# Row maxima of a routed attention in steps of 256 and 512 keys, with VectorE's queue rearranged

## The chip, the core and the metric

The kernel runs on one core of one Trainium2 chip. The metric is the device time of one execution in microseconds (us). A core has five engines that run their own queues side by side: TensorE (PE in the profile, its weight loads PEld), VectorE (DVE), ScalarE (ACT), GpSimd (POOL) and SyncE (SP, which starts transfers). They meet at semaphores. TensorE writes its results into PSUM, eight banks of 512 float32 for each of the 128 partitions; VectorE and ScalarE read PSUM and may write it.

## The reference

Two blocks follow each other. The first is an attention over 4 batches of 8 heads with 768 positions of 64 values, in which a query sees only the keys that were assigned to the same one of 16 clusters:

```python
q_assign = np.argmax(np.einsum('bhsd,hcd->bhsc', q_n, c_n), axis=-1)
k_assign = np.argmax(np.einsum('bhsd,hcd->bhsc', k_n, c_n), axis=-1)
mask = q_assign[:, :, :, None] == k_assign[:, :, None, :]
scores = scale * np.matmul(q, k.transpose(0, 1, 3, 2))
scores = np.where(mask, scores, -1000000000.0)
scores = scores - np.max(scores, axis=-1, keepdims=True)
attn = np.exp(scores)
attn = attn / (np.sum(attn, axis=-1, keepdims=True) + 1e-09)
return np.matmul(attn, v).astype(np.float32)
```

The second takes the result as 3072 tokens of 512 values and computes `h = x @ w_in` (512 to 2048), `g = h * erf(softplus(h))` and `g @ w_out`. The change touches the attention alone.

## The kernel before

The 32 heads are worked as 16 pairs (`p` = 0 to 15), two heads side by side in the partitions 0 to 63 and 64 to 127. A pair has 12 units: two halves of 384 queries, each with six blocks `j` of 128 keys. A unit takes scores (keys by queries) in float32, adds mask and shift, takes the exponential and multiplies by v. `period(p, i)`, line 1345, with `i` = 0 to 5, issues the work of two units `u` and `u + 1`, and between them the preparations of later pairs. Periods 0 to 2 are the first half of the queries, 3 to 5 the second. All engines' instructions keep the order in which the program issues them, so the order of the calls in `period` is the order of every queue.

What runs in a period, with the names that the profile shows:

- `step_ahead(u)` (line 1332) runs the first of two steps of the row maxima of a coming half, `maxima_step` (463). A step takes 128 queries `t` of both heads against half of the 768 keys: two bf16 passes on TensorE into the two banks of the tile `wide` (`wide<-kv,qv`, then the mask `wide<-km,qm`), then one reduction on VectorE, `nmx<-wide`. Both steps use the same `wide`, so each waits until VectorE has read the one before. The second step of a period, `step_ahead(u + 1, True)`, is a generator: its first pass stands behind the products, its mask pass between the two units' `scores`.
- `products(u)` (514) multiplies q and k in float32 into a score bank pair, `sc<-qT,kT`; there are two such pairs, for u and u + 1. `scores(u)` (527) adds mask and shift, `sc<-qm,km`; `curve(u)` (541) takes the exponential on ScalarE, `pr<-sc`.
- `attend(w)` (562) multiplies the exponentials of the two units before by v, `turned<-pr,in_v`, 16 matmuls a unit, into the first 386 columns of `turned[0]` (first half) or `turned[1]` (second half). `accumulate` (550) sums the exponentials on GpSimd.
- `divide` (575), after a half's last unit (at the end of periods 0 and 3): TensorE sums over the keys into the other `turned` bank (`turned<-more_out,minus`), ScalarE makes the inverse (`inv`, twice), VectorE refines it (`den`), scales the two parts of the result (`turned<-turned,inv`, twice, here raw 0 and raw 1), makes the output `x` (`more_out<-den,turned`), and SyncE stores it. It is a generator, `part[0]`, moved on by `next` in the period that follows.
- Routing of pair p + 2: in period 3, `similarities` (394) multiplies by the centroids into `turned[1]` (`turned<-...,ccT`), then `choose` (407), a generator in `routing[0]`, works on VectorE: transposition `sims<-turned`, maximum over the 16 clusters `mx` (384 values to 24; before, into the columns 488 to 511 of the score bank of unit u + 1: `sc<-sims`), comparison `hot<-sims,sc`, and the transpositions `aside` and `hotT`.
- `masks` (437) spreads the clusters of the next pair by a matmul with `pick` into a `turned` bank and copies them to `qm` and `km`; `turn` (494) puts the row maxima in.
- A weight tile of the second block is made a pair at a time between: `size`, `rest` and `sign` on ScalarE, `bounded` and `shifted` on VectorE (`w_in<-w_in` or `w_out<-w_out`), `summed` on GpSimd.

The tiles of the result of `attend` and of the maximum of `choose` are made and taken so:

```python
turned = [ps.tile([P, 512], F32, name=f"turned{i}") for i in range(2)]   # line 172
mx = (wide[:, 0] if spare is None else spare)[:, 512 - n :]              # line 417
```

After the attention (about 408 us) the second block runs to the end; it has no part in the change.

Of the kernel before, what the change touches and what calls it, by code (L numbers as in the profile page):

```python
# [14 lines left out]
ALU = mybir.AluOpType  # L15
ACT = mybir.ActivationFunctionType
AX = mybir.AxisListType
PSUM = bass.MemoryType.PSUM

P = 128  # L20
B, H, S, D = 4, 8, 768, 64
# [4 lines left out]
HW = S // 2  # L26
QW = HW // 2
TW = QW + 1
HJ = NJ // 2
HP = H // 2  # L30
NPAIR = B * HP
DM, DFF = H * D, 2048
NFT = DFF // P
# [9 lines left out]
BIG = 2.0**60  # L43
# [3 lines left out]
N_LATE = 4  # L47
PLACE_OF = [n % 5 for n in range(25)] + [2, 3, 2]
LAST_X = 11
MASKS = {(0, 2): ("k", 0), (2, 0): ("q", 0), (2, 2): ("k", 1), (5, 2): ("q", 1)}  # L50
FIRST_MASKS = {(2, 0): ("k", 0), (2, 1): ("q", 0), (2, 2): ("k", 1), (5, 2): ("q", 1)}

KAPPA = {1: (0, 1), 2: (0, 0), 0: (1, 1), 3: (1, 0)}
# [93 lines left out]
def kernel(  # L147
# [24 lines left out]
    turned = [ps.tile([P, 512], F32, name=f"turned{i}") for i in range(2)]  # L172
# [149 lines left out]
    def bounded(n):  # L322
        w = w_steps[n][0]
        ve.tensor_scalar(out=w, in0=w, scalar1=2.0, scalar2=None, op0=ALU.max)

    def sign(n):
        hi, _, upper = steps[n]
        ae.activation(out=upper, in_=hi, func=ACT.Prelu, scale=2.0**-25, alpha=2.0**90)

    def shifted(n):  # L330
        w = w_steps[n][0].bitcast(U32)
        ve.tensor_scalar(out=w, in0=w, scalar1=3, scalar2=None, op0=ALU.logical_shift_left)
# [8 lines left out]
    for e in range(2):  # L341
        for n in range(2):
            r = e * D + n * Q
# [90 lines left out]
        if p < NPAIR:  # L434
            ae.copy(out=pairs[p][nm + "v"], in_=pairs[p][nm + "T"])

    def masks(p, nm, half, bank, narrow=False, copied_by=ae):

        if p >= NPAIR:
            return lambda: None  # L440
        st = pairs[p]
        cols = slice(half * HW, (half + 1) * HW)
        r, hot = slice(0, D) if nm == "q" else slice(D, P), st["hotT"]
        picked = pick[r, half]
        if narrow:
            r = slice(r.start + Q, r.stop)
            picked = pick[r, 1]
            hot = hot if half else st["aside"]
        won = bank[:, 0:HW]
        te.matmul(won, lhsT=picked, rhs=hot[r], start=True, stop=True)  # L450
        if nm == "q":
            return lambda: ae.activation(out=st["qm"][:, cols], in_=won, func=ACT.Relu)
        if copied_by is ve:
            return lambda: ve.tensor_scalar(
                out=st["km"][:, cols], in0=won, scalar1=BIG, scalar2=nbig, op0=ALU.mult, op1=ALU.add
            )
        return lambda: ae.activation(
            out=st["km"][:, cols], in_=won, func=ACT.Identity, bias=nbig, scale=BIG
        )
# [3 lines left out]
    def maxima_step(p, i, sm=wide, behind=False):  # L463

        st = pairs[p]
        nmx = maxima[p % 2]
        t, half = divmod(i, 2)

        def passes(a, b, start, rows):
            for e in range(2):  # L470
                r = slice(e * D + rows.start, e * D + rows.stop)
                te.matmul(
                    sm[:, e, 0:HW], lhsT=st[a][r, t * P : (t + 1) * P],
                    rhs=st[b][r, half * HW : (half + 1) * HW], start=start, stop=not start,
                )

        passes("qv", "kv", True, slice(0, D))
        if behind:
            yield
        passes("qm", "km", False, slice(Q, D) if behind else slice(0, D))  # L480
        if behind:
            yield
        ve.tensor_reduce(
            out=nmx[:, :, t, half], in_=sm[:, :, 0:HW], axis=AX.X, op=ALU.max, negate=True
        )
        if i in (NJ - 1, 2 * NJ - 1):
            h = i // NJ
            ve.tensor_reduce(
                out=lowest[h][:, :, ::D].rearrange("p t e -> p e t"),
                in_=nmx[:, :, h * HJ : (h + 1) * HJ], axis=AX.X, op=ALU.min,  # L490
            )
            turns.append((p, h))
# [21 lines left out]
    def products(u):  # L514
        p, half, j = units[u]
        if u in sc_of:
            return
        st = pairs[p]
        sc = sc_of[u] = ps_s.tile([P, 2, 512], F32, name="sc", tag="s")
        for e in range(2):  # L520
            r = slice(e * D, (e + 1) * D)
            te.matmul(
                sc[:, e, 0:HW], lhsT=st["kT"][r, j * P : (j + 1) * P],
                rhs=st["qT"][r, half * HW : (half + 1) * HW], start=True, stop=False,
            )
# [49 lines left out]
    def divide(u):  # L575

        p, half, _ = units[u]
        st = pairs[p]
        av = st["av", half]

        psum = turned[1 - half][:, 0:QW]
        for g in range(4):
            te.matmul(psum[g * Q : (g + 1) * Q], lhsT=minus, rhs=st["acc", half][:, g], start=True, stop=True)

        if u + 1 < len(units):
            inv = routep.tile([P, QW], F32, name="inv")
            den = routep.tile([P, QW], F32, name="den")
        else:
            inv, den = part_of(0, 4 * HW, QW), part_of(1, 0, QW)
        ae.activation(out=inv, in_=psum, func=ACT.Ln, bias=alleps, scale=-1.0)  # L590
        ae.activation(out=inv, in_=inv, func=ACT.Exp, scale=-1.0)
        yield
        ve.scalar_tensor_tensor(
            out=den, in0=psum, scalar=S * EPS, in1=inv, op0=ALU.subtract, op1=ALU.mult
        )
        for k in range(2):
            raw = av[:, k, 0:QW]
            ve.scalar_tensor_tensor(
                out=raw, in0=raw, scalar=av[:, k, QW : QW + 1], in1=inv, op0=ALU.add, op1=ALU.mult
            )  # L600
        yield
        x = part_of(0, (2 * p + half) % 4 * HW, HW).rearrange("p (k x) -> p k x", k=2)
        ve.scalar_tensor_tensor(
            out=x, in0=den.unsqueeze(1).to_broadcast([P, 2, QW]), scalar=2.0, in1=av[:, :, 0:QW],
            op0=ALU.add, op1=ALU.mult,
        )
        b, r = divmod(p, HP)
        for g in range(4):
            rows_of, at = r * P + g // 2 * D, b * S + half * HW + g % 2 * QW
            nc.sync.dma_start(  # L610
                out=x_dram[rows_of : rows_of + D, at : at + QW].rearrange("(k r) x -> r k x", k=2),
                in_=x[g * Q : (g + 1) * Q],
            )
        if half == 1:
            del pairs[p]
        yield
# [715 lines left out]
    def step_ahead(u, behind=False):  # L1332
        p, i = divmod(u + NJ, 2 * NJ)
        steps = maxima_step(p, i, behind=behind) if p < NPAIR else iter(())
        if not behind:
            run(steps)
        return steps
# [7 lines left out]
    def period(p, i):  # L1345
# [4 lines left out]
        def mask(place):  # L1350
            which = (MASKS if p else FIRST_MASKS).get((i, place))
            if which:
                return masks(p + 1, *which, turned[0 if i in (0, 5) else 1], place > 1, ve if i == 0 else ae)
            return lambda: None

        if u > 0:
            for which in turns if i in (0, 3) else ():
                turn(*which)
                turns.remove(which)
            step_ahead(u)  # L1360
        mask(0)()
        next(part[0], None)
        if i == 5:
            next(routing[0], None)
# [2 lines left out]
        if u == 2:  # L1367
            next(routing[0])
        products(u)
        products(u + 1)  # L1370
        mask(1)()
        second = step_ahead(u + 1, True) if u > 0 else iter(())
# [1 line left out]
        rows = D if u == 0 or u + NJ >= len(units) else Q  # L1374
        scores(u, rows)
        next(second, None)
        if i:
            next(second, None)
        next(part[0], None)
        scores(u + 1, rows)  # L1380
        later = mask(2)
        if i == 0:
            later()
            later = lambda: None
            next(second, None)
        if i == 3:
            similarities(p + 2)
            routing[0] = choose(p + 2, sc_of[u + 1][:, 0], True)
        curve(u)
        later()  # L1390
        curve(u + 1)
# [8 lines left out]
        if i == 0 and early(n1 - 1):  # L1400
            bounded(n1 - 1)
            shifted(n1 - 1)
            sign(n1 - 1)
        elif i == 1 and early(n1):
            size_and_rest(n1)
        elif i == 3 and early(n1):
            bounded(n1)
            sign(n1)
        elif i == 5 and early(n2):
            rest(n2)  # L1410
        for _ in range(min(len(forms), FORMS.get(p, {}).get(i, 0))):
            forms.pop(0)[0]()
        if i == 3:
            next(routing[0], None)
            if early(n1):
                shifted(n1)
            for _ in range(2):
                next(routing[0], None)
        elif i == 1:
            load(p + 1, "v", v, vp)  # L1420
            if p == 0:
                run(routing[0])
                transposes(2, "q")
        elif i == 2:
            transposes(p + 2, "k")
        elif i == 4:
            vectors(p + 2, "k")
            vectors(p + 2, "q")
        elif i == 5:
            transposes(p + 3, "q")  # L1430
# [222 lines left out]
```

## Time and profile before

| | us |
|---|---|
| median of 3 runs (959.59 to 960.75) | 959.68 |
| the profiled execution, own time | 959.94 |
| its span, first to last instruction | 958.1 |
| the attention, 18 to 408 us of the span | 390.00, of it PE busy 389.26, DVE 330.22, ACT 295.33, POOL 317.90 |
| the second block, 408 to 958 us | 550.00, of it PE busy 546.26 |
| one pair, 250.56 to 275.21 and 275.21 to 299.68 us | 24.65 and 24.47, PE busy all of it |
| granted TensorE clock | 1.00 |

The span is counted from the first to the last instruction; the execution's own time is 1.8 us longer. A busy PE in this table means that a matmul was under way somewhere in the array; several run side by side in its row groups of 32 or 64 rows, and one may wait while another ends, so small waits don't show as idle time but as a wider distance between starts. The windows of 250.56, 275.21 and 299.68 us are the starts of three period 3s. The periods' lengths in the pair from 250.56 us, by the starts of their first `wide<-kv,qv`: period 3 4.91 (4.73 in most pairs), period 4 3.82, period 5 3.92, period 0 4.09, period 1 3.83, period 2 4.09.

### The profile page before, as it was taken

What the parts mean: (1) busy time and instruction counts of PE and PEld (TensorE: products, weight loads), DVE (VectorE), ACT (ScalarE), POOL (GpSimd) and SP (SyncE); (2) the same over time, 40 slices, a digit from 0 to 9 for tenths busy, and PEclk for the clock granted to TensorE, in tenths of its full rate; (3) what the DMA queues carried; (4) which work ended last, traced back from release to release, by engine and by line L of the source; (5) the groups of instructions that cost most, each with busy time, mean ns of one, the idle gap of its engine ahead of it and who ended that gap; (6) DMA issues with size and microseconds to landing.
All of it is one profiled execution on the core that took longest, in us unless ns stands there. A gap on an engine that the chain in (4) does not pass through costs nothing.

```text
span 958.1 us, 22447 instructions
## 1 busy us (share of the span) xinstructions
PE 950.1 (99%) x8954; PEld 728.2 (76%) x8954; DVE 798.0 (83%) x1395; ACT 539.0 (56%) x815; POOL 538.7 (56%) x375
## 2 busy tenths in 40 slices
PE   8999999999999999999999999999999999999998
PEld 3555555555555555588888888998999899989987
DVE  8888888888888887787689889788868987897887
ACT  3777777777777777542524531654257236625541
POOL 1688888778888888897669910360054016202600
PEclk9999999999999999999999999999999999999999
DMA  9345545544454522041403454463445336343533
GB/s 224 61 112 112 112 111 112 112 112 111 90 117 84 132 56 56 22 152 55 177 1 154 154 164 138 135 202 110 155 125 174 115 128 210 110 149 119 157 115 110
DMA packets 172313, 116.06 MB, mean 121 GB/s; under 512 B 131376, under 2 KB 141104, under 8 KB 172208
## 3 DMA queue, kind: packets, MB, share of 16 engines
q1 hardware_dynamic: 169280, 113.41, 42.3%
q8 instruction: 71, 1.16, 0.5%
q10 hardware_dynamic: 2928, 1.21, 0.4%
q14 instruction: 34, 0.28, 0.1%
HBM read 90.21 MB, written 24.38 MB: 120 GB/s over the span
## 4 chain that ended last, share of the span: by engine, by line
PE 95%; DVE 2%; ACT 1%; DMA 1%; issue 0%; DVEq 0%; SPq 0%; ACTq 0%
PE bank L138 41%; PE turned L138 32%; PE sc L138 17%; PE wide L138 6%; DVE nmx L138 1%; DMA out_dram<-osb 0%; ACT a_s L138 0%; DVE osb L138 0%; ACT L138 0%; DVE g L138 0%; DMA in_q<-in_q_dram 0%; DVE g_more L138 0%; DVE kT L138 0%; DVE sims L138 0%; DVE qT L138 0%
## 5 line engine op out<-in xcount | busy, mean ns | idle before, releaser
L138 POOL TENSOR_TENSOR more_out<-more_out,pr 128x768 f32<-128x768 f32 x128 | 217.3, 1698 | 16.2 <-ACT pr L138 6.7
L138 DVE TENSOR_REDUCE nmx<-wide 128x2 f32<-128x768 f32 x189 | 180.5, 955 | 46.4 <-PE wide L138 45.9
L138 ACT ACTIVATE pr<-sc 128x768 f32<-128x768 f32 x192 | 148.7, 810 | 87.2 <-PE wide L138 68.6
L138 POOL TENSOR_TENSOR g<-g 128x512 f32<-128x512 f32 x36 | 47.2, 1310 | 216.6 <-DVE g L138 214.7
L138 PE MATMUL turned<-pr,in_v 128*32 128x193 f32 x3072 | 144.8, 330 | 0.0
L138 PEld LDWEIGHTS turned<-pr,in_v 128*32 128x32 f32 x3072 | 91.5, 109 | 50.7 <-issue 21.3
L138 PE MATMUL sc<-qT,kT 64*128 64x384 f32 x528 | 98.3, 486 | 0.0
L138 DVE TENSOR_TENSOR g<-g 128x512 f32<-128x512 f32 x114 | 79.0, 693 | 15.2 <-PE bank L138 11.7
L138 DVE TENSOR_TENSOR g<-a_s,g 128x512 f32<-128x512 f32 x80 | 73.5, 944 | 5.6 <-ACT a_s L138 5.6
L138 DVE TENSOR_TENSOR g<-bank,g 128x256 f32<-128x256 f32 (+1 forms) x129 | 63.8, 522 | 15.3 <-PE bank L138 8.1
L138 PE MATMUL bank<-w_out,g 128*128 128x256 f32 x328 | 75.4, 379 | 0.0
L138 ACT ACTIVATE a_s<-g 128x1024 f32<-128x1024 f32 (+1 forms) x36 | 41.0, 1149 | 55.9 <-POOL g L138 45.3
L138 PE MATMUL bank<-g_more,g 128*128 128x256 f32 x304 | 71.8, 379 | 0.0
L138 PE MATMUL bank<-x_own,w_in 128*128 128x128 f32 (+1 forms) x432 | 71.6, 308 | 0.0
L138 POOL TENSOR_TENSOR more_out<-pr,pr 128x768 f32<-128x768 f32 x32 | 58.9, 1839 | 20.1 <-ACT pr L138 20.1
L138 PEld LDWEIGHTS bank<-w_out,g 128*128 128x128 f32 x328 | 62.3, 190 | 8.5
L138 PEld LDWEIGHTS <-qv 64*128 64x128 bf16 x384 | 26.9, 93 | 53.4 <-issue 37.3
L138 PEld LDWEIGHTS sc<-qT,kT 64*128 64x128 f32 x528 | 49.2, 187 | 21.9 <-ACT inv L138 3.1
L138 ACT ACT_TABLE_LOAD x40 | 51.3, 1283 | 24.4 <-DVE g L138 23.7
L138 PE MATMUL wide<-kv,qv 64*128 64x384 bf16 x378 | 63.9, 328 | 1.1 <-ACT km L138 0.6
L138 PEld LDWEIGHTS bank<-x_own,w_in 128*128 128x128 f32 x432 | 61.1, 191 | 4.0 <-issue 0.6
L138 PEld LDWEIGHTS bank<-g_more,g 128*128 128x128 f32 x304 | 57.8, 190 | 7.9
(242 smaller groups left out, 2065.3 us busy)
## 6 DMA issues: line engine op xcount, KB each, us to landing
g_more<-b_dram SPq DMA_DIRECT2D x48, 512.0 KB, 3.5
g_more<-w_dram SPq DMA_DIRECT2D x84, 256.0 KB, 2.8
x_own<-in_moe_w_in_dram SPq DMA_DIRECT2D x13, 512.0 KB, 5.4
in_v<-in_v_dram SPq DMA_DIRECT2D x32, 192.0 KB, 3.3
x_dram<-more_out SPq DMA_DIRECT2D x128, 48.0 KB, 1.7
x_own<-x_dram SPq DMA_DIRECT2D x6, 1024.0 KB, 5.4
in_k<-in_k_dram SPq DMA_DIRECT2D x59, 96.0 KB, 2.7
in_q<-in_q_dram SPq DMA_DIRECT2D x58, 96.0 KB, 4.9
```

Source lines behind the costliest of these rows:

```text
L138: ins = getattr(self.engine, name)(*args, **kw)
```

## The change

The 768 keys of a row are no longer cut at 384. For the rows `t` = 0, 1, 3 and 4 the first step takes 256 keys and the second 512, for `t` = 2 and 5 they take 352 and 416. Work moves in VectorE's queue: the copy of one mask (`km`, period 0) goes to ScalarE, raw 1 of the division goes behind the second maximum, the comparison `hot` goes from period 3 to period 4, `bounded` in period 3 behind the transposition `sims`. On ScalarE, `sign` of period 0 goes ahead of the period's exponentials. One mask matmul of period 2 goes from ahead of the products to between them. The maximum `mx` of `choose` is put into `turned[0]`, columns 488 to 511, in place of the score bank.

```diff
+KEYS = (S - 512, S - 512, 352)
...
-MASKS = {(0, 2): ("k", 0), (2, 0): ("q", 0), (2, 2): ("k", 1), (5, 2): ("q", 1)}
+MASKS = {(0, 2): ("k", 0), (2, 3): ("q", 0), (2, 2): ("k", 1), (5, 2): ("q", 1)}
...
-    def masks(p, nm, half, bank, narrow=False, copied_by=ae):
+    def masks(p, nm, half, bank, narrow=False):
...
-        if copied_by is ve:
-            return lambda: ve.tensor_scalar(
-                out=st["km"][:, cols], in0=won, scalar1=BIG, scalar2=nbig, op0=ALU.mult, op1=ALU.add
-            )
         return lambda: ae.activation(
             out=st["km"][:, cols], in_=won, func=ACT.Identity, bias=nbig, scale=BIG
         )
...
         t, half = divmod(i, 2)
+        first = KEYS[t % HJ]
+        keys = (slice(0, first), slice(first, S))[half]
+        n = keys.stop - keys.start
...
                 te.matmul(
-                    sm[:, e, 0:HW], lhsT=st[a][r, t * P : (t + 1) * P],
-                    rhs=st[b][r, half * HW : (half + 1) * HW], start=start, stop=not start,
+                    sm[:, e, 0:n], lhsT=st[a][r, t * P : (t + 1) * P],
+                    rhs=st[b][r, keys], start=start, stop=not start,
                 )
...
-            out=nmx[:, :, t, half], in_=sm[:, :, 0:HW], axis=AX.X, op=ALU.max, negate=True
+            out=nmx[:, :, t, half], in_=sm[:, :, 0:n], axis=AX.X, op=ALU.max, negate=True
...
                 out=raw, in0=raw, scalar=av[:, k, QW : QW + 1], in1=inv, op0=ALU.add, op1=ALU.mult
             )
-        yield
+            if k == 0:
+                yield
...
-                return masks(p + 1, *which, turned[0 if i in (0, 5) else 1], place > 1, ve if i == 0 else ae)
+                return masks(p + 1, *which, turned[0 if i in (0, 5) else 1], place == 2)
...
+            if i == 0 and early(n1 - 1):
+                sign(n1 - 1)
             step_ahead(u)
         mask(0)()
+        if i == 4:
+            next(routing[0], None)
         next(part[0], None)
...
         products(u)
+        mask(3)()
         products(u + 1)
         mask(1)()
...
         next(second, None)
-        if i:
-            next(second, None)
+        next(second, None)
         next(part[0], None)
         scores(u + 1, rows)
         later = mask(2)
         if i == 0:
             later()
             later = lambda: None
-            next(second, None)
         if i == 3:
             similarities(p + 2)
-            routing[0] = choose(p + 2, sc_of[u + 1][:, 0], True)
+            routing[0] = choose(p + 2, turned[0], True)
...
         if i == 0 and early(n1 - 1):
             bounded(n1 - 1)
             shifted(n1 - 1)
-            sign(n1 - 1)
...
         elif i == 3 and early(n1):
-            bounded(n1)
             sign(n1)
...
         if i == 3:
             next(routing[0], None)
             if early(n1):
+                bounded(n1)
                 shifted(n1)
-            for _ in range(2):
-                next(routing[0], None)
+            next(routing[0], None)
```

## The prediction

> **What bounds the kernel now.** I read the page first, then the chain of waits and the two engines' timelines of one pair of heads. The page:
>
> ```profile
> PE 950.1 (99%) x8954; PEld 728.2 (76%) x8954; DVE 798.0 (83%) x1395; ACT 539.0 (56%) x815; POOL 538.7 (56%) x375
> ...
> PE 95%; DVE 2%; ACT 1%; DMA 1%; issue 0%; DVEq 0%; SPq 0%; ACTq 0%
> ```
>
> TensorE is busy 99% of the span and is 95% of the chain that ended last. So a microsecond counts only if it shortens TensorE's stream or makes TensorE wait; work taken from VectorE (83%) counts for nothing by itself. TensorE in period 3 of one pair (its timeline):
>
> ```profile
> 275.21 0.34 PE L138 MATMUL wide<-kv,qv 64*128 64x384 bf16 x2
> 275.38 0.33 PE L138 MATMUL wide<-km,qm 64*128 64x384 bf16 x2
> 275.55 1.45 PE L138 MATMUL sc<-qT,kT 64*128 64x384 f32 x8
> 276.84 0.33 PE L138 MATMUL wide<-kv,qv 64*128 64x384 bf16 x2
> 277.10 0.33 PE L138 MATMUL sc<-qm,km 32*128 32x384 bf16 x2
> 277.10 0.34 PE L138 MATMUL wide<-km,qm 32*128 32x384 bf16 x2
> 277.27 0.32 PE L138 MATMUL sc<-qm,km 32*128 32x384 bf16 x2
> ...
> 278.19 1.49 PE L138 MATMUL turned<-pr,in_v 128*32 128x193 f32 x32
> 279.50 0.51 PE L138 MATMUL turned<-more_out,minus 128*32 128x192 f32 x8
> 279.94 0.34 PE L138 MATMUL wide<-kv,qv 64*128 64x384 bf16 x2
> ```
>
> Read the starts. The first maxima pass takes 0.17 us to the next start, so does the mask pass. At 277.10 the mask pass of the second step starts together with the first unit's scores: they lie in different row groups. The `attend` matmuls start at 278.19, 2.98 after the period's start, the next period 1.75 later. VectorE in the same time (its timeline):
>
> ```profile
> 277.54 0.96 DVE L138 TENSOR_REDUCE nmx<-wide 128x2 f32<-128x768 f32 x1 [0.83 <-PE wide L138]
> 278.42 0.42 DVE L138 TENSOR_SCALAR w_out<-w_out 128x512 f32<-128x512 f32 x1
> 278.75 0.58 DVE L138 STREAM_TRANSPOSE sims<-turned 128x384 f32<-128x384 f32 x1
> 279.25 0.38 DVE L138 TENSOR_SCALAR w_out<-w_out 128x512 uint32<-128x512 uint32 x1
> 279.55 0.55 DVE L138 TENSOR_REDUCE sc<-sims 128x24 f32<-128x384 f32 x1
> 280.13 0.55 DVE L138 TENSOR_TENSOR hot<-sims,sc 128x384 bf16<-128x384 f32 x1
> ```
>
> The cluster maximum (`sc<-sims`) ends at 280.10, long after `attend` has begun; TensorE doesn't care now.
>
> **Steps of 256 and 512 keys.** At 384 keys a pass costs 0.16 to 0.17, that is 0.42 ns a column. In the first step both passes shorten by 128 columns: 2 x 0.053 less. In the second step the first pass grows by 0.053; its mask pass grows too, but runs beside two `scores` that take 277.10 to 277.52 together, so it costs nothing; if that cover were gone, it would cost 0.053. Net 0.053 less for a 256/512 row tile, a quarter of it (0.013) for 352/416. From the second tile of the first pair's second half on there are 61 of the one and 31 of the other: 61 x 0.053 + 31 x 0.013 = 3.6 us less. (The first pair's first four tiles run their steps one after the other at the start; the columns are the same, I take 0.)
>
> On VectorE a reduction of 768 values takes 0.955 and one of 384 0.547, so some 1.06 ns a value: 512 would take 0.69, 1024 1.22, and the sum is unchanged. The second reduction ends 0.27 later than now and the first step of the next period waits for it. In a plain period it starts 2.33 after the period's start and would end at 3.55, with the next start due at 3.71 (3.76 less 0.05): 0.16 spare. Cost 0; without this cover each 0.1 in the four such periods of a pair is 6 us (0.1 x 61).
>
> **Moves that only rearrange.** The mask copy (0.62 on VectorE, 14 times) goes to ScalarE, where a like copy takes 0.57. With `sign` (1.36, though the next starts 1.1 after it) also ahead of period 0's two exponentials, these end some 0.8 later; TensorE's second products of period 1 need the score bank, and by the same rows that leaves 0.2 to 0.3. Queued behind them are the two `inv` steps (0.79), which no longer wait behind `sign` and so come some 0.2 earlier. Cost 0. Raw 1 (0.43) behind the second maximum delays `x` (0.54) and its four stores by 0.4; the mask matmul of period 2, which needs `x` gone, moves back by 0.65, which covers it; SyncE's and GpSimd's orders stay, and the stored x is read pairs later. `hot` behind the next period's first maximum frees that one: in period 4 the products and second step lose 0.02 and 0.04 in the chain of waits now:
>
> ```profile
> 275.71 1.29 PE sc L138 x8
> 277.00 0.16 PE wide L138 x2
> ...
> 280.44 1.31 PE sc L138 x8
> 281.75 0.20 PE wide L138 x2
> ```
>
> Period 1 loses 0.03 to 0.09 likewise (3.79 to 3.85 against 3.76). With the backlog moved away I take 0.035 for each of 28 periods: 1.0 less. Bounds 0 and 1.7.
>
> **The cluster maximum in turned[0].** This step sets the sign. In period 3 `turned[0]` is the bank into which `attend` is accumulating. In the changed program as built, the first `turned<-pr,in_v` matmul of that period waits for VectorE's `turned<-sims`; before, it has no VectorE wait there. This stands 14 times, for p = 0 to 13 (later pairs have no pair p + 2). The columns, 0 to 385 and 488 to 511, are disjoint, but tile and bank are one. So TensorE, which now runs `attend` under VectorE's chain, has to wait for the chain's end, and all behind it in TensorE's queue waits too: 32 matmuls, the 8 of the division, the next period.
>
> The chain, after the period's start: the second reduction starts at 2.33 (277.54 - 275.21; the shorter first and longer second step cancel here) and ends at 3.55. An instruction starts some 0.09 before the recorded end of the one ahead if it needs no result of it: `sims` 3.46, then 0.50 to the next start (278.75 to 279.25), `bounded` 3.96 to 4.38, `shifted`, which needs its result, 4.43, `mx` 0.30 after that (279.25 to 279.55), 4.73, for 0.55: 5.28. From the end of a VectorE instruction to the waiting matmul it is 0.05 (reduction ended 252.29, `wide<-kv,qv` started 252.34). `attend` starts at 5.33 in place of 2.98 - 0.05 = 2.93: a wait of 2.40. In p = 0 no weight tile is made in period 3, so `bounded` and `shifted` are missing: `mx` ends at 4.82 (`sims` 3.56, 0.70 between their starts there, 0.56), a wait of 1.94. Sum 13 x 2.40 + 1.94 = 33.1. Nothing takes it back: from `attend` to the next period's start it is 1.75 of TensorE's own work, and TensorE has no idle time in later periods to make up with. What comes late next is only TensorE's own stream; VectorE, ScalarE and GpSimd get 2.4 of slack. Bounds: 2.2 (an end overlapped as the others are) to 2.65 (0.1 each at the two waits), 30.5 to 36.5.
>
> The rule that speaks against this change stands in the Trainium skill, "PSUM — Partial Sum Buffer", section Terms: two engines must not be on the same bank and quadrant at once, one writing by TensorE and the other reading or writing. By that rule the wait can't be dropped although the columns are disjoint, and the sum stays at 988.2; by the columns alone it would be the last rival's 955.1. The trace of before shows the same pairing once: with `mx` in the score bank, the weight loads of period 4's second products sit idle 13 times, 4.4 in all, until just after `hot` has ended.
>
> ```profile
> PEld sc L138 <- ACT inv L138: 4.4, 13, 0.3
> ```
>
> (The row names ScalarE; `hot` ended at 256.21, that load started at 256.33.)
>
> **Sum.** 959.94 (span 958.1 and 1.84 around it) + 33.1 - 3.6 - 1.0 = 988.4; the runs' median lies 0.26 below the profiled execution, so 988.2 on their scale.
>
> **Rivals.**
> - The steps don't pay: the longer mask pass isn't hidden or the 1.22 reduction holds up the next period. For it: 0.16 spare is little. Against: row groups start independently at 277.10, and VectorE enters period 4 without backlog. Price 0.053 x 61 = 3.2 and the 1.0: 992.4. Chance 0.13.
> - TensorE's clock falls after each wait. For it: in the trace's first 3.4 us of matmuls the distance between 256-column passes is 0.21, twice the later one, so there is a slow state at the start. Against: an idle 0.56 at 11.67 changed nothing; the longest wait is 2.4. Price: 16 distances in the start took 3.39 in place of 1.70, so 1.7 for each of 14: 24 us, 1012. Chance 0.05. The Trainium skill, "TensorE: Matmul & The Clock Gate", part 1, has the clock halved after an idle window of about 3.4 us; by that rule 2.4 is too short. No trace here has such a gap in the middle.
>
> ```profile
> 2.40 3.78 PE L138 MATMUL turned<-pick,identb 128*128 128x256 bf16 x17 [2.40 <-DVE alleps L138]
> ```
>
> - Not slower: the wait in period 3 falls on something that is done, as it would if `mx` came ahead of 2.93. Then only the gains are left: 959.7 - 4.6 = 955.1. It decides from where the wait is under 4.6 / 14 = 0.33 a pair, `mx` ended by 3.2. Against: `mx` needs `sims`, which needs the centroid matmuls that stand just ahead of `attend` in TensorE's own queue (277.52 to 278.37), plus 0.58 and 0.55 on VectorE, so 4.3 at the very least even on an idle VectorE. Chance 0.03, of which 0.01 lies within 0.2%.
>
> **How the numbers follow.** The forecast has 0.79, the rivals 0.13, 0.05 and 0.03. Predicted is the likeliest, 988.2. The range holds the forecast's bounds (30.5 - 5.3 and 36.5 - 3.6 on 959.7: 984.9 to 992.6) and the first rival at the longer wait (36.5 on 959.7: 996); a little below for reductions faster than the line gives: 984 to 996. It leaves out clock and no wait, 0.08, and the edges. Slower by over 0.2% (1.9 us, about what a measurement of this kernel tells from no change) 0.97, within 0.01, faster 0.02.
>
> **What would show it.** In the changed profile: `turned<-pr,in_v` of period 3 starts some 5.3 after the period's start, with an idle time before it of 2.4 put down to VectorE's `turned` or `sims`, 14 times; TensorE busy share of the attention falls by 33 us; pairs 14 and 15 run 0.24 a pair shorter than before; other periods shrink by 0.05 to 0.1; granted clock 1.00. I am wrong if `attend` starts near 2.9, or if waits before `wide<-kv,qv` come up in periods 0, 1 and 4.

## The result and the profile after

The changed kernel takes 999.69 us (median of 5 runs, 998.28 to 1002.26) beside 960.75 us (959.59 to 961.15) for the kernel before: a ratio of 1.0414, interval 1.0395 to 1.0434. It is slower, as forecast, but by 39 us and not by 28; the forecast of 988.2 and its range of 984 to 996 miss it.

The page of the changed kernel, engines and chain:

```profile
PE 961.2 (96%) x8954; PEld 719.7 (72%) x8954; DVE 795.7 (80%) x1381; ACT 554.0 (55%) x829; POOL 537.8 (54%) x375
...
PE 89%; DVE 7%; issue 2%; ACT 1%; DMA 1%; DVEq 0%; ACTq 0%
```

TensorE still has the same 8954 matmuls, but 39 us of the span lie outside its busy time (1000.5 - 961.2; before 958.1 - 950.1 = 8), and VectorE now holds 7% of the chain that ended last. Where this happens is seen in period 3 of one pair. VectorE's timeline (start, duration, engine, line, operation, output and input):

```profile
277.38 0.65 DVE L139 TENSOR_REDUCE nmx<-wide 128x2 f32<-128x512 f32 x1
279.15 1.23 DVE L139 TENSOR_REDUCE nmx<-wide 128x2 f32<-128x1024 f32 x1 [1.12 <-PE wide L139]
280.30 0.57 DVE L139 STREAM_TRANSPOSE sims<-turned 128x384 f32<-128x384 f32 x1
280.79 0.85 DVE L139 TENSOR_SCALAR w_out<-w_out 128x512 f32<-128x512 f32 x2
281.55 0.56 DVE L139 TENSOR_REDUCE turned<-sims 128x24 f32<-128x384 f32 x1
```

and TensorE's, from the period's start at 276.87:

```profile
276.87 0.28 PE L139 MATMUL wide<-kv,qv 64*128 64x256 bf16 x2
276.99 0.27 PE L139 MATMUL wide<-km,qm 64*128 64x256 bf16 x2
277.10 1.46 PE L139 MATMUL sc<-qT,kT 64*128 64x384 f32 x8
278.39 0.38 PE L139 MATMUL wide<-kv,qv 64*128 64x512 bf16 x2
...
279.13 0.85 PE L139 MATMUL turned<-more_out,ccT 128*32 128x384 f32 x8
282.16 1.51 PE L139 MATMUL turned<-pr,in_v 128*32 128x193 f32 x32 [2.17 <-DVE turned L139]
283.49 0.51 PE L139 MATMUL turned<-more_out,minus 128*32 128x192 f32 x8
283.93 0.28 PE L139 MATMUL wide<-kv,qv 64*128 64x256 bf16 x2
```

The cluster maximum `turned<-sims` ends at 282.11, and `attend` (`turned<-pr,in_v`) starts 0.05 later, 5.29 after the period's start; the forecast had 5.33. The idle time before it, 2.17, is counted from the end of the centroid matmuls. The period takes 7.06 us in place of 4.73. Over the whole execution this group of matmuls waited 14 times (the group's line, then its line in the view of waits: us in total, times, longest):

```profile
L139 PE MATMUL turned<-pr,in_v 128*32 128x193 f32 x3072 | 151.5, 340 | 29.8 <-DVE turned L139 29.8
...
PE turned L139 <- DVE turned L139: 29.8, 14, 2.2
```

What was not forecast stands in every third pair. In five of the 14 pairs period 3 took 8.50 to 8.65 us, and there the clock fell. A table of stretches around one of them, with the columns length, busy time and count of PE, PEld, DVE, ACT and POOL, then the granted clock, the share of the DMA engines and GB/s:

```profile
305.20:308.61 3.41, 1.62 (x18) 0.27 (x14) 2.59 (x5) 2.60 (x3) 1.37 (x1) 1.00 0.98 235
308.61:312.02 3.41, 3.03 (x40) 1.77 (x40) 0.33 (x1) 0.14 (x1) 3.06 (x2) 0.50 0.65 104
312.02:315.43 3.41, 3.41 (x52) 1.79 (x48) 2.69 (x5) 2.28 (x5) 0.00 (x0) 1.00 0.30 47
```

The same two groups of matmuls as above, in this stretch of clock 0.50:

```profile
308.99 2.80 PE L139 MATMUL turned<-pr,in_v 128*32 128x193 f32 x32 [2.17 <-DVE turned L139]
311.57 0.72 PE L139 MATMUL turned<-more_out,minus 128*32 128x192 f32 x8
312.23 0.28 PE L139 MATMUL wide<-kv,qv 64*128 64x256 bf16 x2
```

`attend` takes 2.80 in place of 1.51: the clock is at half for exactly one stretch of 3.413 us behind the wait, and then whole again.

The profiled execution of the changed kernel took 1002.26 us (the longest of its five), the one of before 959.94: 42.3 more. The lengths of all periods in the two traces, from one period's first `wide<-kv,qv` to the next one's, summed by their number in the pair, put it where it belongs (the forecast's terms are spread over the periods they name). The last pair prepares no maxima after its period 2, so its periods 2 to 5 are one row:

| | before, us | after, us | difference | forecast |
|---|---|---|---|---|
| period 0 | 63.15 | 66.09 | +2.9 | -0.8 |
| period 1 | 61.15 | 60.52 | -0.6 | -1.3 |
| period 2 | 61.70 | 61.66 | 0.0 | -0.2 |
| period 3 | 70.58 | 109.80 | +39.2 | +32.3 |
| period 4 | 57.17 | 55.72 | -1.5 | -1.3 |
| period 5 | 58.83 | 58.83 | 0.0 | -0.2 |
| start, to period 0 of the first pair | 20.23 | 20.78 | +0.6 | 0 |
| last pair, periods 2 to 5 | 15.13 | 15.11 | 0.0 | 0 |
| second block | 550.21 | 551.95 | +1.7 | 0 |
| sum of the differences | | | +42.3 | +28.5 |

### The profile page after: what moved, and what is told of

Its sections match the earlier page's. It is cut to its first block, busy times and chain, and to the rows that moved or that the text cites. A ratio compares the mean times of both kernels' runs of the same rounds, so it can differ in the third digit from the quotient of the medians.

```text
span 1000.5 us, 22391 instructions
## 1 busy us (share of the span) xinstructions
PE 961.2 (96%) x8954; PEld 719.7 (72%) x8954; DVE 795.7 (80%) x1381; ACT 554.0 (55%) x829; POOL 537.8 (54%) x375
## 4 chain that ended last, share of the span: by engine, by line
PE 89%; DVE 7%; issue 2%; ACT 1%; DMA 1%; DVEq 0%; ACTq 0%
PE bank L139 37%; PE turned L139 30%; PE sc L139 16%; PE wide L139 6%; DVE nmx L139 2%; DVE g L139 1%; DVE sims L139 1%; ACT a_s L139 1%; DVE turned L139 1%; DVE w_in L139 1%; DVE w_out L139 1%; ACT L139 1%; DMA out_dram<-osb 1%; DVE g_more L139 0%; DVE osb L139 0%
## 5 line engine op out<-in xcount | busy, mean ns | idle before, releaser
L139 DVE TENSOR_REDUCE nmx<-wide 128x2 f32<-128x512 f32 (+1 forms) x189 | 179.4, 949 | 93.3 <-PE wide L139 90.5
L139 PE MATMUL turned<-pr,in_v 128*32 128x193 f32 x3072 | 151.5, 340 | 29.8 <-DVE turned L139 29.8
L139 PE MATMUL wide<-kv,qv 64*128 64x256 bf16 (+1 forms) x378 | 65.0, 328 | 1.2 <-DVE nmx L139 0.7
L139 PE MATMUL wide<-km,qm 64*128 64x256 bf16 (+1 forms) x378 | 62.5, 326 | 0.0
L139 PEld LDWEIGHTS sc<-qT,kT 64*128 64x128 f32 x528 | 46.6, 187 | 19.6 <-ACT pr L139 3.9
```

Source lines behind the costliest of these rows:

```text
L139: ins = getattr(self.engine, name)(*args, **kw)
```

## The experiments

### The cluster maximum alone, and taken out of the bank

Three kernels ask whether the bank of the maximum is the cause. The first puts this one line into the kernel before (`e2_before_mx_turned`):

```diff
-            routing[0] = choose(p + 2, sc_of[u + 1][:, 0], True)
+            routing[0] = choose(p + 2, turned[0], True)
```

> The kernel before with one edit: mx in turned[0], nothing else of the change. There hot still follows mx in period 3 and reads the same bank, so attend waits for hot. Theory A: hot ends 5.47 after the period's start, attend starts at 5.52 in place of 2.98, 2.54 in 13 pairs and 2.2 in the first, 35 us, and the clock falls after some of the waits, each 1.5: 1002 to 1008, granted clock under 0.995. Rival B (the clock falls for another reason, such as the passes of 512 columns): 996, clock 1.000. Rival D (tile order does not matter, the wait of the changed kernel comes from its other moves): 961.

Measured: 1001.12 us (999.99 to 1003.14), just under the 1002 to 1008 of theory A, ratio 1.0418 [1.0401, 1.0436], mean clock 0.991 to 0.994. One line costs as much as the whole change. Here `hot` still stands in period 3, and TensorE waits for it:

```profile
L138 PE MATMUL turned<-pr,in_v 128*32 128x193 f32 x3072 | 150.6, 339 | 32.8 <-DVE hot L138 32.8
```

The second is the changed kernel with the maximum in a tile of its own in SBUF (`e1_mx_sbuf`):

```diff
-        mx = (wide[:, 0] if spare is None else spare)[:, 512 - n :]
+        mx = routep.tile([P, n], F32, name="mx")
```

> The changed kernel with the cluster maximum mx in a tile of its own in SBUF, not in turned[0]; nothing else moved. Theory A (the wait of attend for mx, 32 us, and the clock that falls after some of these waits, 7.5 us, are what the change cost; period 0 adds 2.7 and period 4 gives 1.5 back): attend of period 3 starts at 2.9 after the period's start again, granted clock 1.000, time near 961 (959 to 963). Rival B (the waits cost the 33 of the forecast alone, and the 11 above it come from the other moves and from reductions of 1024): 968 to 972. Rival C (it costs something of its own to compare from SBUF): not under 965.

Measured: 965.80 us (964.85 to 966.47), ratio 1.0054 [1.0039, 1.0069], clock 1.00. The wait is gone, `attend` starts at 2.93 again and period 3 takes 4.68. But 961 was missed by 5, in periods 4 and 5. The timelines of GpSimd and VectorE in this kernel:

```profile
259.51 1.29 POOL L139 TENSOR_TENSOR w_out<-w_out,x_own 128x512 int32<-128x512 int32 x1 [2.17 <-ACT x_own L139]
```

```profile
260.10 1.12 DVE L139 TENSOR_TENSOR hot<-sims,mx 128x384 bf16<-128x384 f32 x1
261.14 0.34 DVE L139 SCALAR_TENSOR_TENSOR den<-turned,inv 128x192 f32<-128x192 f32 x1
```

With `mx` in PSUM `hot` takes 0.54 or 0.55 beside the same GpSimd sum (`e5_mx_behind_attend` below); with both inputs in SBUF it takes 1.12, of which 0.70 pass before GpSimd's sum ends at 260.80. The first pair has no such sum, and there `hot` takes 0.55 from SBUF too:

```profile
36.82 0.55 DVE L139 TENSOR_TENSOR hot<-sims,mx 128x384 bf16<-128x384 f32 x1
```

So rival C's time came out, but the price is not that of reading SBUF; it is that of doing so beside GpSimd. Everything behind `hot` on VectorE is late, and in the 13 other pairs periods 4 and 5 grow to 3.96 and 4.06 (3.71 and 3.92 in the changed kernel): 0.39 x 13 = 5.1.

The third leaves the maximum in `turned[0]`, but issues it behind `attend` (`e5_mx_behind_attend`, against the changed kernel):

```diff
                 bounded(n1)
                 shifted(n1)
-            next(routing[0], None)
...
             for w in (u - 2, u - 1):
                 attend(w)
+            if i == 3:
+                next(routing[0], None)
```

> The changed kernel with one call moved: mx of choose is issued behind attend of period 3, not ahead of it, so that mx (still in turned[0], still at the same place of VectorE's queue) waits for attend and not attend for mx. Theory A (the order of these two on one bank is what cost the 32 us of waits and, through them, the 6 to 7.5 us of the clock): attend of period 3 starts at 2.9, the clock is 1.000, period 4 at 3.7, period 5 at 3.92, period 0 still at 4.28; 959.5 to 963. Rival B (the 11 above the forecast came from the other moves): 968 to 972. In the first of these experiments the comparison hot took 1.12 in place of 0.55 with both operands in SBUF; here it takes 0.55 again.

Measured: 959.51 us (959.25 to 960.02, 11 runs), ratio 0.9997 [0.9988, 1.0006], clock 1.00. The whole loss is gone and no gain is left over. TensorE and VectorE of its period 3, which starts at 275.63:

```profile
278.56 1.49 PE L139 MATMUL turned<-pr,in_v 128*32 128x193 f32 x32
279.86 0.51 PE L139 MATMUL turned<-more_out,minus 128*32 128x192 f32 x8
280.30 0.28 PE L139 MATMUL wide<-kv,qv 64*128 64x256 bf16 x2
```

```profile
279.55 0.84 DVE L139 TENSOR_SCALAR w_out<-w_out 128x512 f32<-128x512 f32 x2
280.31 0.55 DVE L139 TENSOR_REDUCE turned<-sims 128x24 f32<-128x384 f32 x1
280.77 0.68 DVE L139 TENSOR_REDUCE nmx<-wide 128x2 f32<-128x512 f32 x1
```

`attend` starts 2.93 after the period's start, without a wait. It ends at 280.05, and VectorE comes to the maximum at 280.31 anyway: the order of the two on the bank is turned round, and the wait that remains costs nobody anything. So the price was neither the tile nor the columns, but the order in which two engines were sent to one bank. The wait stands in the program as it was built; what the chip would do without it no run here shows.

### The clock

Two kernels keep the wait and shorten TensorE's idle time in it. Filler matmuls of 100 columns go between the centroid matmuls and `attend`, 20 of them (`e3_after_filled`) or 10 (`e8_fill10`):

```diff
             similarities(p + 2)
+            if p + 2 < NPAIR:
+                for _ in range(FILL):
+                    te.matmul(
+                        turned[0][:, 388:488], lhsT=identb, rhs=zeros[:, 0:100],
+                        start=False, stop=False, skip_group_check=True,
+                    )
             routing[0] = choose(p + 2, turned[0], True)
```

> The changed kernel with 20 extra matmuls of 100 columns (zeros, added onto columns of turned[0] that nobody reads) between the centroid products and attend in period 3 of the 14 pairs, so that TensorE idles about 1 us or less there in place of 2.17, while attend waits as long as before. Theory A: granted clock 1.000, attend of period 3 still at 5.3 and the next period at 7.06 in every pair, time shorter by 4 or 5 falls of the clock at 1.5: 991 to 994. Rival B (the fall of the clock costs nothing or has another cause): unchanged, 998 to 1002.

> The changed kernel with 10 extra matmuls in the wait of period 3 in place of 20: TensorE idles some 1.65 to 1.7 in each of 14 periods, attend as late as before. In the two kernels with falls of the clock, a fall stood behind every stretch of 3.41 us (they lie on a fixed raster) with 1.74 us of idle or more, and behind none with 1.69 or less. Theory A (about half such a stretch idle decides): no fall, clock 1.000, 993 to 994.5. Rival (any idle time over some 1.2 may bring a fall, more likely the longer it is): 2 to 4 falls, 995 to 1000.

Measured: 993.64 us (993.32 to 993.98), ratio 1.0344 [1.0329, 1.036], with 20, and 993.72 (993.58 to 993.87), ratio 1.0353 [1.0339, 1.0367], with 10. Period 3 keeps its 7.06 us in both, so the wait as such is untouched, and the clock stays whole:

```profile
core 0: 991.9 us, clock 1.000
```

(the clock by core of the first; the second has the same line). The idle time before `attend` is 1.18 and 1.62 in place of 2.17:

```profile
277.27 1.51 PE L140 MATMUL turned<-pr,in_v 128*32 128x193 f32 x32 [1.62 <-DVE turned L140]
```

(TensorE's timeline of the kernel with 10.) The clock's falls cost 6 us by the medians; by the profiled executions period 3 adds up to 109.80 in the changed kernel and 102.31 with 20 fillers: 7.5 for five falls, 1.5 each. The mean clock of the changed kernel's five runs is 0.991 to 0.993; a fall takes 3.413 x 0.5 / 1000.5 = 0.0017 from it, so by estimate four or five falls a run, and its times scatter by 4 us where those of the filled kernels scatter by less than 1.

The table's every third pair can be worked out too. A pair of the changed kernel takes 26.83 us by the medians of its six periods; three of them and one fall take 3 x 26.83 + 1.5 = 82.0, and 24 stretches of 3.413 take 81.9, so the wait comes back to the same place among the stretches. In `e2_before_mx_turned` a pair takes 26.95; four and one fall take 109.3, 32 stretches 109.2, and its last four falls are 32 stretches apart.

### The steps of 256 and 512 keys

They were put into the kernel before, alone (`e4_before_keys`), and taken out of the version without the wait (`e7_384_keys`, against `e5_mx_behind_attend`). The first edit is the `KEYS` part of the change in `maxima_step`, the second is:

```diff
-KEYS = (S - 512, S - 512, 352)
+KEYS = (HW, HW, HW)
```

> The kernel before with the steps of 256 and 512 (352 and 416) keys alone, VectorE's queue as it was. TensorE alone would give 3.6 us less: 957. Theory A: VectorE's order does not fit the longer second reduction: in period 0 the km copy holds it and the next period starts about 0.25 late, in periods 1 and 4 up to 0.1: 959 to 963. Rival: the longer mask pass is not hidden beside the scores, then no gain anywhere: 963 to 966.

> The first kernel of this group with 384 keys in every step, all moves kept: what the steps of 256 and 512 are worth in the new order. Theory A: they give 0.05 in periods 3, 4 and 2 by 0.013, nothing in periods 0 and 1, which ScalarE sets, and cost 0.5 in the start and 1.3 in the second block: 959 to 963, within 1.5 us of the first kernel of this group. Rival (the steps pay on TensorE everywhere, 3.6): 3 us and more above it.

Measured: alone 967.49 us (966.16 to 968.12), ratio 1.0070 [1.0055, 1.0085]; without the steps 960.64 (960.27 to 960.76), ratio 1.0008 [0.9999, 1.0016], 1.1 more than with them (959.51). In VectorE's old order the steps cost 7, more than either expectation had: periods 0, 2, 3 and 4 grow to 4.30, 4.19, 4.94 and 3.84 (4.09, 4.09, 4.73 and 3.82 before), and only period 1 shrinks (3.71). In period 0 the trace shows why: the second reduction stands behind the mask copy on VectorE and, 1.22 long now, ends 4.25 after the period's start (4.02 before), 0.05 ahead of the next period. For the other three it wasn't followed up. In the new order they gain 1.1 (0.6 by the profiled executions): 0.05 in each of periods 3 and 4, less 0.3 at the start and 0.5 in the second block. So the steps need the rearranged queue; together the two are worth nothing that can be measured in `e5_mx_behind_attend`.

### Period 0

In the changed kernel period 0 is 0.19 longer than before, 4.28 to 4.09. ScalarE and TensorE in one of them, which starts at 291.56 (timeline of all engines):

```profile
293.25 1.38 ACT L139 ACTIVATE x_own<-x_own 128x512 int16<-128x512 f32 x1
...
294.65 0.58 ACT L139 ACTIVATE km<-turned,nbig 128x384 bf16<-128x384 f32 x1
...
295.13 1.50 ACT L139 ACTIVATE pr<-sc 128x768 f32<-128x768 f32 x2
295.35 0.19 PEld L139 LDWEIGHTS turned<-more_out,minus 128*32 128x32 f32 x8 [0.33 <-issue]
295.38 0.53 PE L139 MATMUL turned<-more_out,minus 128*32 128x192 f32 x8
```

The first line is `sign`. It starts before the mask's matmul (at 293.63) is ready, and the next instruction starts 1.40 later (1.39 to 1.41 in all 14 pairs; in the kernel before, where `inv` came next, it was 1.07 to 1.09). The mask copy `km` behind it ends at 295.23, and only then do the division's matmuls write into the same `turned` bank: they start 1.50 behind `attend` (at 293.88), where it was 1.33 before. The exponentials behind `km` are late as well, and in period 1 the weight loads of the second products wait for them (view of waits, before, then changed):

```profile
PEld sc L138 <- ACT pr L138: 0.3, 1, 0.3
PEld sc L139 <- ACT pr L139: 5.9, 15, 0.4
```

Two kernels take `sign` away from there, both against `e5_mx_behind_attend`. In the first (`e6_sign_period1`) `sign` goes behind the two `inv` steps of period 1, and GpSimd's `summed`, which needs it, to period 2:

```diff
-            if i == 0 and early(n1 - 1):
-                sign(n1 - 1)
             step_ahead(u)
         mask(0)()
+        if i == 1 and early(n1 - 1):
+            sign(n1 - 1)
...
-            if i == 1 and early(n1 - 1):
+            if i == 2 and early(n1 - 1):
                 summed(n1 - 1)
```

> The one before, and sign of period 0 goes behind the two inv steps of period 1 (summed of the same weight tile from period 1 to 2). Theory A: the mask copy km then runs at once behind turn's copies, the division's matmul no longer waits for it, the exponentials end 0.9 earlier: period 0 from 4.28 to 4.04 to 4.10, period 1 from 3.78 to 3.71: 3.5 to 4.3 us less than the one before, 956 to 959. Rival: period 0 is held by something else (the longer second step on VectorE), then no difference over 1 us.

Measured: 967.65 us (967.36 to 967.82), ratio 1.0081 [1.0068, 1.0095]. Period 0 takes 4.09 again, so the cause of its 0.19 is shown. But in seven pairs, 8 to 14, the next period grew to between 5.34 and 5.36; in pairs 1 to 7 it takes 3.71. All engines' timeline in one of the seven:

```profile
269.09 1.82 POOL L139 TENSOR_TENSOR more_out<-pr,pr 128x768 f32<-128x768 f32 x1 [0.27 <-DVE w_out L139]
269.13 2.06 DVE L139 TENSOR_SCALAR w_out<-w_out 128x512 uint32<-128x512 uint32 x1
...
271.84 0.39 PE L139 MATMUL wide<-kv,qv 64*128 64x512 bf16 x2 [1.47 <-DVE nmx L139]
```

GpSimd, no longer held back here by `summed` (which needs the shifted tile), starts its accumulation 0.04 before VectorE's `shifted`; that takes 2.06 in place of 0.43 and ends only after GpSimd's 270.91. The row maximum behind it is late, and TensorE waits 1.47. In pairs 1 to 7 `shifted` falls into period 0 with no GpSimd instruction beside it, and takes 0.43. The second kernel (`e9_sign_behind_inv`) is the same with `summed` left in period 1, so that GpSimd must wait for `sign` and stays out of the way.

> The edit of e6 with GpSimd's sum of the weight tile left in period 1 (it now waits for sign and so keeps GpSimd still while VectorE shifts). Computes all of the reference. Theory (in e6 the shift was long because GpSimd's accumulation of the exponentials ran beside it; without that the late sign frees the mask copy and costs nothing): period 0 4.09 as in e6, shifted back at 0.4 us, period 1 3.78 or less with no maximum above 3.9; 14 x 0.19 = 2.7 less than e5: 956 to 958, which would be below the kernel before (959.7). Rival A (the shift is long for another reason, for example because both its operands lie in SBUF whoever else runs): shifted still near 2 us, 967 again. Rival B (GpSimd, which must now wait for sign until about 6 us after the start of period 0, falls behind with the accumulations and the exponentials of the next units find no free tile): the exponentials of period 1 and 2 wait for GpSimd and period 2 grows above 4.2: 960 to 964.

Measured: 963.91 us (963.86 to 964.04), ratio 1.0043 [1.003, 1.0057]: rival B came out in the sum, though not at its place. Period 0 takes 4.09, period 1 3.71 and `shifted` 0.43, as the theory had it (so rival A is out), and the wait for the exponentials is gone from period 1. But period 3 takes 5.21 (4.68), 7.7 more over all pairs. GpSimd and TensorE in these timelines:

```profile
272.33 1.30 POOL L139 TENSOR_TENSOR w_out<-w_out,x_own 128x512 int32<-128x512 int32 x1 [2.30 <-ACT x_own L139]
273.59 1.82 POOL L139 TENSOR_TENSOR more_out<-pr,pr 128x768 f32<-128x768 f32 x1
```

```profile
282.53 0.53 PE L139 MATMUL turned<-more_out,minus 128*32 128x192 f32 x8 [0.33 <-POOL more_out L139]
```

GpSimd waits 2.30 for `sign`, its accumulations come late, and the division at the end of the half waits for their sum. No version that was tried beats the kernel before by more than the measurement tells.

## Why the prediction was right in sign and wrong in size

- **The cluster maximum in turned[0]: right, to the step.** Forecast was `attend` at 5.33 and a wait of 2.40, 14 times; measured 5.29 and 5.29 - 2.93 = 2.36, in the first pair 4.64 in place of 4.87. Without the clock's falls, that is with the fillers, period 3 is 31.7 longer than before; forecast was 33.1 - 0.8. The wait belongs to that one line: alone it costs 40 us, and moved behind `attend` nothing. The program as built keeps the two engines apart on the shared bank although the columns are disjoint; whether the chip needs that wait was not tried.
- **TensorE's clock falls after each wait: this rival was put aside wrongly.** It had 0.05 because "the longest wait is 2.4" and an idle 0.56 had changed nothing. Measured were five falls behind 14 waits, 7.5 us in the profiled execution and 6 by the medians with and without fillers. So the sum had nothing for a cost that was there. The rival's own price, 1.7 for each of 14, was near in size (1.5) and wrong in number: only waits that lie well in a fixed raster make the clock fall. The falls are over half of the 11.5 us by which the median misses the forecast.
- **Moves that only rearrange, "Cost 0": wrong in period 0.** The step took `sign` to hold ScalarE for 1.1 and looked for the delay at the exponentials. That 1.1 was read where `inv` came next; ahead of `km` it was 1.40, and the first to be late was the division, which needs the mask copy gone from its bank: 0.19 in each of some 14 pairs, and with the gain of the shorter passes that it swallowed 3.7 of difference to the forecast. The exponentials were late as well: of the 0.2 to 0.3 that the step left for them nothing remained, and period 1 takes 3.78 where it takes 3.71 with `sign` moved away. `e6_sign_period1` and `e9_sign_behind_inv` show the cause.
- **"Steps of 256 and 512": mis-sized.** The term was -3.6; in the new order they gave -1.1. The gain of 0.05 a period was there in periods 3 and 4, lost behind `sign` in period 0 and behind the late exponentials in period 1, and paid back with 0.3 at the start, which the forecast took as 0. The rival "The steps don't pay" saw the size, not the place: nothing held up periods 3 and 4. In VectorE's old order the steps do cost, 7 us.
- **The small waits: right.** Period 4 fell by 0.11, a little over the 0.05 + 0.035 forecast. Period 1 fell by 0.01 only, for the reason above; with 384 keys in the new order (`e7_384_keys`) periods 1 and 4 together are 1.5 shorter over all pairs than before, where the term had 1.0 and bounds of 0 and 1.7.
- **Not forecast, and open.** The second block is 1.7 longer though nothing in it changed. It was 551.2 to 552.0 long in the changed kernel, with fillers, with the maximum in SBUF and with the steps alone, and 549.8 to 550.3 in the others. At one place some 13 us behind the attention's end VectorE's `w_out` step takes 1.2 to 1.5 in these five traces and 0.41 or 0.42 in the other six. Why it does so in some and not in others stays open. The later start alone isn't the reason: `e5_mx_behind_attend` starts as late as `e1_mx_sbuf` (first `attend` at 25.19 and 25.18) and has 550.3 where that has 551.6.

The terms together: 28.5 forecast, and to it 7.5 for the clock, 3.7 for period 0, 2.3 for start and second block, 1.0 in periods 1, 2 and 5, less 0.7 in periods 3 and 4 (without the clock), make the 42.3 measured in the profiled execution.

## What to carry to other kernels

A small result that was put into the free columns of a bank into which TensorE was accumulating cost TensorE the whole chain ahead of that result; issued behind the accumulation, the same bank was free of charge, because VectorE came to it later anyway. Ask for each tile that you move who is sent to its bank next, and in which order. Price a wait of TensorE not only by its length: look at how much of a clock stretch it fills (here 1.74 us of one was enough). And before a step is moved on an idle engine, ask for each of its neighbours what it had been keeping apart: a `sign` that came later left VectorE's shift beside GpSimd's accumulation in one version and GpSimd late for the division in the other.

## What the runs showed of the hardware

- **Half a stretch idle is enough for the clock.** Counted back from the falls in steps of 3.413 us, TensorE was idle (no matmul under way in the trace) 2.17, 2.06, 1.90, 1.78 and 1.74 us in the five stretches ahead of the changed kernel's falls, and at most 1.58 in all others of the attention. With the one line in the kernel before, falls stood behind 2.16, 2.05, 1.98, 1.96 and 1.95, none behind 1.69, 1.62 or 1.59. So in these two traces the bound lies between 1.69 and 1.74, about half a stretch. With 10 fillers the gap is 1.62, below the bound wherever it lies, and no fall came. The Trainium skill, "TensorE: Matmul & The Clock Gate", part 1, has a free-running window of 3413 ns and the lower clock after a whole idle one. The length and the fixed raster agree with these traces; the whole idle window doesn't, a gap of 2.17 was enough where it lay well.
- **GpSimd holds VectorE up on some forms.** `hot` with two inputs in SBUF took 1.12 beside a GpSimd instruction (0.55 with none beside it, and 0.54 or 0.55 beside one when an input was in PSUM) and ended 0.42 after it; `shifted`, with one input, took 2.06 (0.43 with none beside it) and ended 0.28 after GpSimd's. The Trainium skill, "SBUF — State Buffer", section Who interferes with whom, states that the one that starts second is blocked until the first is done, for VectorE instructions with two SBUF inputs and for the two-port modes that `tensor_scalar` can enter. Both traces agree, and both times the blocked one was on the path to TensorE.
